# Ten of sixteen rows of summed mixing weights made in DRAM by copies and adding transfers, and one attention product tied to the end of z2

## The chip, the cores and the metric

The kernel runs on one core of a Trainium2 chip. A core has five engines that run their own instruction queues: TensorE (PE in the profile; its weight loads are PEld), VectorE (DVE), ScalarE (ACT), GpSimd (POOL) and SyncE (SP, which here only issues transfers). Transfers (DMA) are issued by SP, ACT or POOL and carried by 16 DMA engines. SBUF is the on-chip memory of 128 partitions, PSUM the accumulators that PE writes, DRAM the memory outside. The metric is the device time of one execution in microseconds, the median of several runs.

## The reference

The input x has 2048 rows of 512. It is normalised by rows to xn, and the result is x + s * silu(b), with

- s, attention: xn @ wqkv gives 32 heads of 16; each position looks at 8 earlier positions, 2 apart, with a softmax over these 8; the result goes through wo.
- b, a gated unit: z = gelu(xn @ w_in); z1 is its first 896 columns, z2 the other 896, normalised by rows; g = w_sp @ z2 + b_sp, where w_sp is 2048 x 2048 and mixes the rows (the "mixing"); b = (z1 * g) @ w_out.

```
z1 = z[..., :Fh]
z2 = _layernorm(z[..., Fh:], axis=-1)
g = jnp.einsum("ts,bsf->btf", w_sp, z2) + b_sp[None, :, None]
return jnp.einsum("bsf,fd->bsd", z1 * g, w_out)
```

All is float32. The kernel splits each operand of a product into a high and a low part (fp32r) and does three matmuls for one.

## The kernel before, in words

**Stages on PE.** In this order: the products of wqkv (until about 157 us), z1 (until about 226 us), z2 (until about 295 us), the mixing (twelve block products, until about 571 us), the product with w_out, and the product of attention's result with wo. Attention itself is DVE's work (16 units of two steps: scores L573, sums over a head L580, softmax, weighted product L620, folds, a transpose), with one fold on POOL (L633). It is issued at the lowest priority, its DVE instructions in one fixed order (`line`), and fills what the other work leaves free on DVE, from about 100 to 655 us. The scheduler of the framework orders each engine's instructions by priority and by a simulated timeline; `add_manual_dep` adds an edge, either only of order (NOSYNC) or one waited for at run time (SYNC).

**The mixing.** w_sp is cut into blocks of 128 x 512: four column groups c of outputs (512 each) by sixteen row blocks js. Two column groups belong to one half a (c = 2a, 2a + 1). For each half a and each pair of row blocks (i, 8 + i), the four blocks t0, t1 (row block i) and l0, l1 (row block 8 + i) take part in a scheme with seven products in place of eight (Strassen's, in Winograd's form), for which four sums of blocks are needed:

```
s3 = l1 + t1;  s1 = t1 + t0;  s0 = t0 + s3;  s2 = l0 + s0
```

So 2 halves x 8 = 16 rows of four sums. The plain blocks are used by the products m1, m2, m4 (`plain`), the sums by m6 (s0), m7 (s1), m5 (s3) and m3 (s2) (`summed`). They are made ahead and kept in DRAM (`sums_d`), each row by loading its four blocks, four additions (L393) and storing:

- half 1, rows 0 to 5: `pool_sums` on POOL, during the products of wqkv (L486 to L488); loads, additions and stores all on POOL.
- half 0, rows 0 to 7: `first_sums` during z1 (L690 to L715): loads on SP, additions on DVE, stores on POOL, in the t4 tiles.
- half 1, rows 6 and 7: `raw_sums` during z2 (L781): loads and stores on SP, additions on DVE, in the four raw buffers that also take the weights' loads.

**Weights.** `prep` (L175) fetches a block on SP into one of four raw buffers (`RAW = 4`), ACT makes the high part (L195) and DVE the low part (L197), in one of eight pairs of tiles. A raw buffer is free for the fetch four blocks on once the low part is made.

**z2.** For each i of eight, PE makes row blocks i and 8 + i in two halves of columns (`z2_half`, evicted by ACT at L733). One round later `z2_stats` counts mean and variance (DVE L742 to L745), POOL raises to the power -1/2 (L746) and makes the shift (L748); another round later ACT normalises (L754), ACT and DVE split, and `combine` (L767) makes the sums of z2 that the scheme needs.

**The start of the mixing.** m1a uses wsp_0 to wsp_7 of half 0 and z2's row blocks 0 to 7; m1b the same of half 1. Before m1b four PSUM banks get the bias by ACT (`seed`, L843). In `plain` a tie (L864 to L867) puts the tenth weighted product of attention (`sums_of[9]`, L620) on DVE behind the low part of wsp_6 of m1a.

Of the kernel before, what the change touches and what calls it, by code (L numbers as in the profile page):

```python
# [17 lines left out]
P = 128  # L18
# [6 lines left out]
FB = FH // P  # L25
# [3 lines left out]
JC = NT // NC  # L29
HT = NT // 2  # L30
F3 = 3 * P
ODD = 3
# [25 lines left out]
def kernel(  # L58
# [330 lines left out]

    def added(ts, eng):  # L390
        t0, t1, l0, l1 = ts
        for out_, p_, q_ in ((l1, t1, l1), (t1, t0, t1), (t0, t0, l1), (l0, t0, l0)):
            eng.tensor_tensor(out_, p_, q_, op=ALU.add)  # L393

    def block_sums(a, i, tile_=None, eng=nc.vector, loads=nc.sync, stores=nc.scalar, behind=None):
        top, low = [(tile_ or t4)(f"s{n}_{a}_{i}") for n in "ab"]
        for t, r in ((top, 0), (low, HT)):
            ins = loads.dma_start(t, w_sp[2 * a : 2 * a + 2, r + i].rearrange("c p t -> p c t"))
            if behind:
                tc.add_manual_dep(ins.ins, behind[0].ins.name, behind[1], reason="sums later")  # L400
        added([top[:, 0], top[:, 1], low[:, 0], low[:, 1]], eng)
        for r, t in enumerate((top, low)):
            stores.dma_start(sums_d[a, r, i], t)

    def raw_sums(a, i):
        ts = [
            fetch(w_sp[2 * a + c, r + i], CT, f"sr_{a}_{i}_{c}_{r}") for r in (0, HT) for c in range(2)
        ]
        added(ts, nc.vector)
        for n, t in enumerate(ts):  # L410
            nc.sync.dma_start(sums_d[a, n // 2, i, :, n % 2], t)

    def early_tile(name):
        return t2(name).rearrange("p (i t) -> p i t", i=2)

    def pool_sums(a, i, tile_, *behind):
        block_sums(a, i, tile_, nc.gpsimd, nc.gpsimd, nc.gpsimd, behind)

    z1_sums = [(0, i) for i in range(HT)]

# [57 lines left out]
    for j in range(11, NT):  # L478
        if j + 2 < NT:
            fetch_cols(j + 2)  # L480
        if j == NT - 3:
            rb = raws.tile([P, 512], F32, tag="raw", name="rb", bufs=RAW)
            rbv = rb.rearrange("p (j q) -> p j q", j=JC)
            pin(nc.sync.dma_start(rbv, mv_d[:JC, 1].unsqueeze(0).to_broadcast([P, JC, P])))
        turned = column_tile(j)
        if j == 12:  # L486
            for i in range(HT - 2):
                pool_sums(1, i, early_tile, turned, SYNC)  # L488
        low_x(j - 1, cols[j - 1])
        if j % 2:  # L490
            pair(0, j - 5)
# [197 lines left out]

    def first_sums(a, i):  # L690
        block_sums(a, i, stores=nc.gpsimd)

    first_sums(*z1_sums[0])

    for f in range(FB):
        pair_ = side_pair("w1_last") if f == FB - 1 else None
        wh, wl = prep(w_in1[:, f, :], KB * P, f"w1_{f}", pair_=pair_)
        for c in range(NC):
# [9 lines left out]
            zt = zp[:, c % 2]  # L708
            nc.scalar.activation(zt, pz, AF.Gelu_apprx_tanh)  # L709
            if c % 2:  # L710
                nc.scalar.dma_start(z1_d[f, c - 1 : c + 1].rearrange("c p t -> p c t"), zp)
# [13 lines left out]
    def z2_half(j, h, zt):  # L725
        xh, xl = xn_at(j)
        pz = mm(f"z2_{j}_{h}")[:, : WID[h]]
        for k in range(KB):
            wh, wl = [w[:, : WID[h]] for w in w2[k, h]]
            nc.tensor.matmul(pz, xh[:, k], wh, start=k == 0, stop=False)  # L730
            nc.tensor.matmul(pz, xh[:, k], wl, start=False, stop=False)  # L731
            nc.tensor.matmul(pz, xl[:, k], wh, start=False, stop=k == KB - 1)  # L732
        nc.scalar.activation(zt[:, HALF[h]], pz, AF.Gelu_apprx_tanh)  # L733

# [3 lines left out]
    def z2_stats(i, zts):  # L738
# [5 lines left out]
        mean, rstd = [mvz[:, i : i + HT + 1 : HT, n] for n in range(2)]  # L744
        nc.vector.tensor_scalar(rstd, rstd, EPS, None, op0=ALU.add)  # L745
        nc.gpsimd.tensor_tensor(rstd, rstd, nhalf.to_broadcast([P, 2]), op=ALU.pow)  # L746
# [101 lines left out]
    def block_product(a, name, z, w, odd=None, start=False, stop=False, steps=()):  # L848
        for n, s0 in enumerate(range(0, HT, 2)):
# [7 lines left out]
            for do in steps[n] if steps else ():  # L857
                do()

    def plain(a, c, r):  # L860
        def w(s):
            js = r * HT + s
            pair_ = spatial.get((2 * a + c, js)) or spatial_block(2 * a + c, js)
# [4 lines left out]
            return pair_  # L868
# [310 lines left out]
```

## Time and profile before

| | us |
|---|---|
| median of 3 runs | 695.89 (694.54 to 697.04) |
| the profiled execution, its own time | 696.54 |
| its span, first to last instruction | 694.8 |
| PE / DVE / ACT / POOL busy | 686.6 / 619.4 / 277.7 / 215.2 |
| DMA | 182.36 MB, mean 262 GB/s |

In rows of instructions the line, the engine, the operation and the tiles (out<-in) are given, with the start and the duration in us in a timeline, or with count, busy time and mean in a group; what stands in brackets is the idle time of the engine ahead of the instruction and what ended it. "SPq" is the issue of a transfer by SP. A row of waits gives the total, the number of times and the longest. A row of stretches gives the length, then each engine's busy time and number of instructions (PE, PEld, DVE, ACT, POOL), the granted clock, the share of the 16 DMA engines and GB/s. A row of one line's instructions gives the count, the shortest, median and longest duration in ns, and the first and last start. Matmuls overlap in the profile: one of 512 columns is drawn 0.39 us long, though the next starts earlier.

### The profile page before, as it was taken

How to read it: one execution, taken by the hardware profiler on the slowest of the kernel's cores; microseconds unless marked ns; L12 is line 12 of the kernel's file. 1: busy time of each engine (PE TensorE's matmuls, PEld its weight loads, DVE VectorE, ACT ScalarE, POOL GpSimd, SP SyncE). 2: the span in 40 equal slices, each digit the busy share in tenths (PEclk: the TensorE clock that was granted, in tenths of full speed). 3: DMA queues.
4: the chain of work that ended last, by engine and by line, in shares of the span. 5: the costliest groups of instructions: out<-in, count | busy, mean ns of one | idle time of the engine just before them, and what ended most of it. 6: DMA issues, size and time to landing. Idle time of an engine off the chain costs nothing.

```text
span 694.8 us, 9233 instructions
## 1 busy us (share of the span) xinstructions
PE 686.6 (99%) x3084; PEld 573.0 (82%) x3084; DVE 619.4 (89%) x866; ACT 277.7 (40%) x458; POOL 215.2 (31%) x242
## 2 busy tenths in 40 slices
PE   8999999999999999998999999999999999999998
PEld 7888888888888899986888888888888888888886
DVE  6776868999989989889999998999989999989775
ACT  4342234224424256865534544442334444211531
POOL 3104837372343322124123222223111201642320
PEclk9999999999999999999999999999999999999999
DMA  8769899969999865267899768667576692655796
GB/s 270 252 193 289 288 348 384 346 204 358 407 412 340 329 231 190 80 201 231 258 403 314 284 211 298 208 232 248 183 261 206 215 342 89 221 173 190 246 330 235
DMA packets 102223, 182.36 MB, mean 262 GB/s; under 512 B 9184, under 2 KB 45280, under 8 KB 102176
## 3 DMA queue, kind: packets, MB, share of 16 engines
q1 hardware_dynamic: 56624, 102.21, 43.6%
q0 software_dynamic: 13824, 52.24, 20.9%
q10 hardware_dynamic: 31728, 27.33, 11.7%
q8 instruction: 24, 0.39, 0.2%
q14 instruction: 23, 0.19, 0.1%
HBM read 122.42 MB, written 59.32 MB: 262 GB/s over the span
## 4 chain that ended last, share of the span: by engine, by line
PE 67%; DVE 13%; DMA 12%; ACT 3%; issue 3%; POOL 1%; SPq 1%; DVEq 0%; POOLq 0%; ACTq 0%
PE g L825 35%; PE b L1067 4%; PE b L1069 4%; PE b L1068 4%; PE qkv L387 4%; PE qkv L386 4%; PE qkv L385 4%; DMA sb<-in_w_sp 3%; PE s L1069 2%; PE s L1068 2%; PE s L1067 2%; DMA sums_d<-sb 2%; DVE zst L742 2%; DMA z_d<-z1t 1%; DVE xT L280 1%
## 5 line engine op out<-in xcount | busy, mean ns | idle before, releaser
L633 POOL TENSOR_TENSOR pv<-pv 128x1024 f32<-128x1024 f32 x29 | 69.6, 2399 | 96.2 <-DVE pv L620 85.9
L573 DVE TENSOR_TENSOR pr<-k,q 128x2048 f32<-128x2048 f32 x32 | 73.6, 2299 | 2.0 <-DMA k<-qkv_d 1.9
L620 DVE TENSOR_TENSOR pv<-v,lg 128x2048 f32<-128x2048 f32 x32 | 74.6, 2331 | 0.7
L580 DVE TENSOR_REDUCE lg<-pr 128x128 f32<-128x2048 f32 x32 | 73.0, 2281 | 0.1
L647 POOL DMA_DIRECT2D o_d<-tt x32 | 18.0, 562 | 138.9 <-DVE tt L646 103.8
L433 ACT ACTIVATE stage<-qkv 128x512 f32<-128x512 f32 x40 | 23.0, 590 | 30.8 <-DMA qkv_d<-stage 17.0
L807 POOL DMA_DIRECT2D ol<-o_d x32 | 17.7, 555 | 37.7 <-DVE BIG L197 11.1
L1078 ACT ACTIVATE bt<-b 128x512 f32<-128x512 f32 x16 | 9.4, 599 | 43.5 <-PE b L1069 39.4
L709 ACT ACTIVATE z1t<-z 128x512 f32<-128x512 f32 x28 | 15.5, 597 | 26.1 <-DMA z_d<-z1t 15.3
L280 DVE TENSOR_TENSOR xT<-xT,mr 128x512 f32<-128x512 f32 x20 | 14.9, 743 | 11.9 <-DMA mr<-mv_d 6.4
L732 PE MATMUL z<-w_0h,BIG 128*128 128x512 f32 x64 | 25.0, 391 | 0.0
L731 PE MATMUL z<-w_0l,BIG 128*128 128x512 f32 x64 | 25.0, 391 | 0.0
L730 PE MATMUL z<-w_0h,BIG 128*128 128x512 f32 x64 | 24.9, 390 | 0.0
L742 DVE BATCH_NORM_STATS2 zst<-zt 128x6 f32<-128x448 f32 x32 | 19.3, 613 | 6.1 <-ACT zt L733 6.0
L754 ACT ACTIVATE zt<-zt,nmz,mvz 128x896 f32<-128x896 f32 x16 | 17.5, 1129 | 18.0 <-POOL nmz L748 18.0
L638 DVE TENSOR_TENSOR pv<-pv 128x512 f32<-128x512 f32 x32 | 22.9, 716 | 0.0
L733 ACT ACTIVATE zt<-z 128x512 f32<-128x512 f32 (+1 forms) x32 | 15.9, 536 | 15.2 <-DMA sums_d<-sa 14.0
L732 PE MATMUL z<-w_1h,BIG 128*128 128x384 f32 x64 | 21.5, 336 | 0.0
L730 PE MATMUL z<-w_1h,BIG 128*128 128x384 f32 x64 | 21.5, 335 | 0.0
L731 PE MATMUL z<-w_1l,BIG 128*128 128x384 f32 x64 | 21.4, 335 | 0.0
L393 POOL TENSOR_TENSOR sb<-sa,sb 128x512 f32<-128x512 f32 x12 | 19.7, 1644 | 5.4 <-DMA sb<-in_w_sp 5.1
L195 ACT ACTIVATE BIG<-zl 128x512 fp32r<-128x512 f32 x20 | 12.5, 630 | 21.6 <-DVE zl L895 19.8
(478 smaller groups left out, 2296.2 us busy)
## 6 DMA issues: line engine op xcount, KB each, us to landing
qkv_d<-stage ACTq DMA_DIRECT2D x24, 512.0 KB
v<-qkv_d POOLq DMA_DIRECT2D x14, 704.0 KB, 5.4
k<-qkv_d POOLq DMA_DIRECT2D x13, 704.0 KB, 6.8
sums_d<-sa POOLq DMA_DIRECT2D x14, 512.0 KB, 7.8
sums_d<-sb POOLq DMA_DIRECT2D x14, 512.0 KB, 8.0
z_d<-z1t ACTq DMA_DIRECT2D x14, 512.0 KB
zl<-z_d SPq DMA_DIRECT2D x12, 512.0 KB
tr<-t_d SPq DMA_DIRECT2D x12, 384.0 KB
```

The source lines that it names most:

```text
L573: line(nc.vector.tensor_tensor(pr, taps(ks[u], j0), qb.unsqueeze(1).to_broadcast([P, W, NJ * CS]), op=ALU.mult))
L580: line(nc.vector.tensor_reduce(lgs[u][:, j0 * HS : (j0 + NJ) * HS].rearrange("p i w -> p w i"), pr.rearrange("p w (i d) -> p w i d", d=DH) ...
L620: line(nc.vector.tensor_tensor(pv.rearrange("p w (i d) -> p w i d", d=DH), taps(vs[u], j0).rearrange("p w (i d) -> p w i d", d=DH), lgs[u] ...
L633: eng.tensor_tensor(pv[:, 0:4], pv[:, 0:4], pv[:, 4:8], op=ALU.add)
L730: nc.tensor.matmul(pz, xh[:, k], wh, start=k == 0, stop=False)
L731: nc.tensor.matmul(pz, xh[:, k], wl, start=False, stop=False)
L732: nc.tensor.matmul(pz, xl[:, k], wh, start=False, stop=k == KB - 1)
L742: nc.vector.bn_stats(st[:, h], zt[:, h * FQ : (h + 1) * FQ])
L825: nc.tensor.matmul(pg, z[a], w[b], start=start and i == 0, stop=stop and i == 2, skip_group_check=seeded)
L1067: nc.tensor.matmul(pp[:, cols], hi, wh, start=k == 0, stop=False)
L1068: nc.tensor.matmul(pp[:, cols], hi, wl, start=False, stop=False)
L1069: nc.tensor.matmul(pp[:, cols], lo, wh, start=False, stop=k == n - 1)
```

## The change

The six rows on POOL stay (`MINE = 6`). The ten others (half 0, rows 0 to 7; half 1, rows 6 and 7) are made two rows at a time, as five pairs, without SBUF: for each pair four tensors in DRAM of 0.5 MB (`sums_q`), one for each sum. A sum is made by copying one block pair there (`copied`, issued by ACT) and adding another onto it with an adding transfer (`plus`, issued by POOL). `weight_sums` gives the 40 transfers in five rounds over the five pairs; `go_on(1, behind)` issues the next one, tied to the instruction `behind`: a copy by order on ACT alone, an adding transfer by a wait. It is called after each second eviction in z1 (14 times), after each row block of z2 (16 times) and after each pair of blocks in the mixing from m1b on (the last 10, so into m2b). All DVE additions and the SP loads and POOL or SP stores of these rows are gone. The tie of the tenth weighted product to wsp_6 is gone; instead the thirteenth (`sums_of[12]`) stands on DVE behind the last `z2_stats` (L745 of i = 7).

```diff
+MINE = HT - 2
+THEIRS = [(0, q) for q in range(HT // 2)] + [(1, q) for q in range(MINE // 2, HT // 2)]
...
-    sums_d = dram.tile([2, 2, HT, P, 2, CT], F32, name="sums_d")
+    sums_d = dram.tile([2, MINE, P, 2, CT], F32, name="sums_d")
+    sums_q = {
+        (a, n, q): dram.tile([2, P, CT], F32, name=f"sums_{a}_{n}_{q}")
+        for a, q in THEIRS
+        for n in range(4)
+    }
...
+    def rows_of_2k(blocks_):
+        return blocks_.rearrange("s p t -> (s p t)").rearrange("(r x) -> r x", x=4 * CT)
+
+    def raw_blocks(a, n, q):
+        r, c = divmod(n, 2)
+        j = r * HT + 2 * q
+        return w_sp[2 * a + c, j : j + 2]
+
+    def copied(to, a, q, src):
+        return nc.scalar.dma_start(rows_of_2k(sums_q[a, to, q]), rows_of_2k(src(a, q))), NOSYNC
+
+    def plus(to, a, q, src):
+        ins = nc.gpsimd.dma_start(
+            rows_of_2k(sums_q[a, to, q]), rows_of_2k(src(a, q)), accum_op=ALU.add, max_dma_last_dim=2048
+        )
+        return ins, SYNC
+
+    def weight_sums():
+        t0, t1, l0, l1 = [lambda a, q, n=n: raw_blocks(a, n, q) for n in range(4)]
+        s0, s3 = [lambda a, q, n=n: sums_q[a, n, q] for n in (0, 3)]
+        rounds = (
+            ((copied, 3, l1),),
+            ((copied, 0, t0), (plus, 3, t1)),
+            ((plus, 0, s3), (copied, 1, t0)),
+            ((plus, 1, t1), (copied, 2, l0)),
+            ((plus, 2, s0),),
+        )
+        for ops in rounds:
+            for a, q in THEIRS:
+                for fn, to, src in ops:
+                    yield fn, to, a, q, src
+
+    coming_sums = weight_sums()
+
+    def go_on(n, behind):
+        for fn, *args in itertools.islice(coming_sums, n):
+            ins, how = fn(*args)
+            tc.add_manual_dep(ins.ins, behind.ins.name, how, reason="sums paced")
...
-    first_sums(*z1_sums[0])
...
-            nc.scalar.activation(zt, pz, AF.Gelu_apprx_tanh)
+            out_of = nc.scalar.activation(zt, pz, AF.Gelu_apprx_tanh)
             if c % 2:
+                go_on(1, out_of)
                 nc.scalar.dma_start(z1_d[f, c - 1 : c + 1].rearrange("c p t -> p c t"), zp)
-        if f == 2:
-            first_sums(*z1_sums[FB])
-        if f < FB - 1:
-            first_sums(*z1_sums[f + 1])
...
-        nc.vector.tensor_scalar(rstd, rstd, EPS, None, op0=ALU.add)
+        known = nc.vector.tensor_scalar(rstd, rstd, EPS, None, op0=ALU.add)
+        if i == HT - 1:
+            tc.add_manual_dep(sums_of[12].ins, known.ins.name, NOSYNC, reason="gate rows ahead")
...
-        if i in (1, 3):
-            raw_sums(1, HT - 2 + i // 2)
...
-                    z2_half(j, h, zt)
+                    out_of = z2_half(j, h, zt)
+                    if h:
+                        go_on(1, out_of)
...
+            if name != "m1a":
+                go_on(1, highs[-1])
...
-            if (a, c, js) == (0, 0, 6):
-                tc.add_manual_dep(
-                    sums_of[9].ins, lows[-1].ins.name, NOSYNC, reason="first weights ahead"
-                )
...
     def summed(a, half_, i):
-        return lambda s: prep(sums_d[a, half_, s, :, i], CT, f"ws_{a}{half_}{i}_{s}")
+        def w(s):
+            if a and s < MINE:
+                src = sums_d[half_, s, :, i]
+            else:
+                src = sums_q[a, 2 * half_ + i, s // 2][s % 2]
+            return prep(src, CT, f"ws_{a}{half_}{i}_{s}")
+
+        return w
```

More of the change, by code (lines that the diff above doesn't have):

```diff
@@ L388, in product @@
         return pq
[L390 to L411, printed above, removed]
     def early_tile(name):
         return t2(name).rearrange("p (i t) -> p i t", i=2)
-    def pool_sums(a, i, tile_, *behind):
-        block_sums(a, i, tile_, nc.gpsimd, nc.gpsimd, nc.gpsimd, behind)
-    z1_sums = [(0, i) for i in range(HT)]
+    def pool_sums(i, *behind):
+        top, low = [early_tile(f"s{n}_{i}") for n in "ab"]
+        for t, r in ((top, 0), (low, HT)):
+            ins = nc.gpsimd.dma_start(t, w_sp[2:4, r + i].rearrange("c p t -> p c t"))
+            tc.add_manual_dep(ins.ins, behind[0].ins.name, behind[1], reason="sums later")
+        t0, t1, l0, l1 = [top[:, 0], top[:, 1], low[:, 0], low[:, 1]]
+        for out_, p_, q_ in ((l1, t1, l1), (t1, t0, t1), (t0, t0, l1), (l0, t0, l0)):
+            nc.gpsimd.tensor_tensor(out_, p_, q_, op=ALU.add)
+        for r, t in enumerate((top, low)):
+            nc.gpsimd.dma_start(sums_d[r, i], t)
@@ L486 @@
         if j == 12:
-            for i in range(HT - 2):
-                pool_sums(1, i, early_tile, turned, SYNC)
+            for i in range(MINE):
+                pool_sums(i, turned, SYNC)
         low_x(j - 1, cols[j - 1])
@@ L688 @@
     attention()
-    def first_sums(a, i):
-        block_sums(a, i, stores=nc.gpsimd)
-    first_sums(*z1_sums[0])
     for f in range(FB):
@@ L732, in z2_half @@
             nc.tensor.matmul(pz, xl[:, k], wh, start=False, stop=k == KB - 1)
-        nc.scalar.activation(zt[:, HALF[h]], pz, AF.Gelu_apprx_tanh)
+        return nc.scalar.activation(zt[:, HALF[h]], pz, AF.Gelu_apprx_tanh)
     def spatial_block(c, js):
@@ L862, in w @@
             js = r * HT + s
-            pair_ = spatial.get((2 * a + c, js)) or spatial_block(2 * a + c, js)
-            if (a, c, js) == (0, 0, 6):
-                tc.add_manual_dep(
-                    sums_of[9].ins, lows[-1].ins.name, NOSYNC, reason="first weights ahead"
-                )
-            return pair_
+            return spatial.get((2 * a + c, js)) or spatial_block(2 * a + c, js)
         return w
     def summed(a, half_, i):
-        return lambda s: prep(sums_d[a, half_, s, :, i], CT, f"ws_{a}{half_}{i}_{s}")
+        def w(s):
[5 more added lines that the diff above has]
+        return w
     def operand(i, s0):
```

## The prediction

> **What bounds the kernel now.** I read the page's busy times and chain first.
>
> ```profile
> span 694.8 us, 9233 instructions
> PE 686.6 (99%) x3084; PEld 573.0 (82%) x3084; DVE 619.4 (89%) x866; ACT 277.7 (40%) x458; POOL 215.2 (31%) x242
> ...
> PE 67%; DVE 13%; DMA 12%; ACT 3%; issue 3%; POOL 1%; SPq 1%; DVEq 0%; POOLq 0%; ACTq 0%
> ```
>
> TensorE (PE) is busy for 99% of the span and VectorE (DVE) for 89%; but a busy PE can hide gaps, so the next view is the list of PE's waits, and then the stretches of 25 us.
>
> ```profile
> PE g L825 <- ACT g L843: 1.9, 1, 1.9
> ...
> PE g L825 <- ACT BIG L195: 0.2, 1, 0.2
> ```
>
> ```profile
> 300.00:325.00 25.00, 22.89 (x100) 18.36 (x99) 22.84 (x32) 15.18 (x25) 8.34 (x9) 1.00 0.71 226
> 325.00:350.00 25.00, 25.00 (x111) 20.65 (x111) 25.00 (x35) 12.90 (x23) 6.44 (x6) 1.00 0.78 256
> ```
>
> After its opening PE waits in one place: the stretch from 300 to 325 us holds 100 matmuls of 512 columns where the next holds 111. That is where the mixing product begins. The matmuls around the hole:
>
> ```profile
> 314.66 0.39 PE L825 MATMUL g<-wsp_6l,BIG 128*128 128x512 f32 x1
> 314.89 0.39 PE L825 MATMUL g<-wsp_6h,BIG 128*128 128x512 f32 x1
> 317.17 0.50 PE L825 MATMUL g<-wsp_0h,BIG 128*128 128x512 f32 x1 [1.90 <-ACT g L843]
> ...
> 323.88 0.39 PE L825 MATMUL g<-wsp_3h,BIG 128*128 128x512 f32 x1
> 324.48 0.50 PE L825 MATMUL g<-wsp_7h,BIG 128*128 128x512 f32 x1 [0.21 <-ACT BIG L195]
> ```
>
> Starts are 0.23 us apart when PE flows (314.66 to 314.89). The first hole costs 317.17 - 314.89 - 0.23 = 2.05 us, the second 324.48 - 323.88 - 0.23 = 0.37 us, and the first matmul after each runs 0.50 instead of 0.39 us: 2.05 + 0.37 + 2 x 0.11 = **2.64 us**. This is all that any edit behind the opening can win before the last matmul; everything else it touches can at best stay hidden. Note the order: PE did the four products of row block 6, skipped block 7, went on to the second half (wsp_0 to wsp_3), and took wsp_7 at 324.48. The first hole waits for the seeds (L843), the second for z2's row block 7 (L195). What made both late stands on DVE, ScalarE (ACT), the load queue (SP) and GpSimd (POOL):
>
> ```profile
> 303.43 0.69 DVE L197 TENSOR_TENSOR wsp_6l<-wsp_6r,wsp_6h 128x512 fp32r<-128x512 f32 x1 [1.42 <-ACT wsp_6h L195]
> 304.04 2.29 DVE L620 TENSOR_TENSOR pv<-v,lg 128x2048 f32<-128x2048 f32 x1
> 306.24 2.28 DVE L580 TENSOR_REDUCE lg<-pr 128x128 f32<-128x2048 f32 x1
> ...
> 309.29 0.62 DVE L742 BATCH_NORM_STATS2 zst<-zt 128x6 f32<-128x448 f32 x1
> 309.82 0.67 DVE L197 TENSOR_TENSOR wsp_7l<-wsp_7r,wsp_7h 128x512 fp32r<-128x512 f32 x1
> ...
> 318.58 0.16 DVE L745 TENSOR_SCALAR mvz<-mvz 128x2 f32<-128x2 f32 x1
> ```
>
> ```profile
> 303.82 0.47 ACT L733 ACTIVATE zt<-z 128x384 f32<-128x384 f32 x1
> 304.20 0.62 ACT L195 ACTIVATE wsp_7h<-wsp_7r 128x512 fp32r<-128x512 f32 x1
> ...
> 313.99 0.64 ACT L195 ACTIVATE wsp_3h<-wsp_3r 128x512 fp32r<-128x512 f32 x1 [5.03 <-DMA wsp_3r<-in_w_sp]
> ...
> 316.00 0.63 ACT L195 ACTIVATE wsp_5h<-wsp_5r 128x512 fp32r<-128x512 f32 x1
> 316.53 2.14 ACT L843 ACTIVATE g<-b_bh 128x512 f32<-128x512 f32 x4
> 321.22 2.16 ACT L754 ACTIVATE zt<-zt,nmz,mvz 128x896 f32<-128x896 f32 x2 [2.54 <-POOL nmz L748]
> ```
>
> ```profile
> 310.52 0.33 SPq L169 DMA_DIRECT2D wsp_3r<-in_w_sp  x1
> ...
> 312.73 0.33 SPq L169 DMA_DIRECT2D wsp_5r<-in_w_sp  x1
> ```
>
> ```profile
> 318.82 1.68 POOL L746 TENSOR_TENSOR mvz<-mvz,nhalf 128x2 f32<-128x2 f32 x1 [1.83 <-DVE mvz L745]
> ```
>
> The tenth weighted product (L620) is tied behind wsp_6l, and runs at once at 304.04 with L580 behind it: 4.5 us. Meanwhile wsp_7h was done at 304.82, but wsp_7l came only at 309.82, and its raw buffer (there are four) lets wsp_3r start at 310.52, 0.03 us after. So wsp_3h is at 313.99; wsp_5r starts at 312.73, wsp_5h is at 316.00, and the seeds stand behind it on ACT. The same 4.5 us hold z2's last statistics (evicted at 304.29, counted at 309.29), and more attention holds L745 to 318.58.
>
> **The change part by part.** *DVE's sums.* Ten rows of four additions:
>
> ```profile
> L393 DVE TENSOR_TENSOR sb<-sa,sb x16: 627/684/1003, 169.3 to 244.1; 128x512 f32<-128x512 f32 x16
> ```
>
> 40 x 0.684 (the median of the commonest form) = 27.4 us leave DVE. On the path this is 0: PE has no wait there. The time goes to attention, which is next to be late on DVE.
>
> *The loads, stores and buffers of these rows.* SP loses 8 x 2 + 8 + 8 = 32 issues of about 0.33 us (the wsp_3r row), 10.6 us; POOL loses 16 store issues. 0 on the path, for the same reason.
>
> *Copies and adding transfers.* 40 of 0.524 MB: 20 copies issued by ACT, 20 adding ones by POOL, each pair of rows 4 + 4. Nearest rows for an issue:
>
> ```profile
> L711 ACTq DMA_DIRECT2D z_d<-z1t x14: 366/366/367, 160.6 to 223.3; - x14
> ...
> L403 POOL DMA_DIRECT2D sums_d<-sa x14: 532/545/589, 70.1 to 241.6; - x14
> ```
>
> ACT gains 20 x 0.366 = 7.3 us; by the order of the generator 10 copies fall in the z1 stage, 7 in z2, 3 later. POOL gains 20 x 0.545 and loses 16 x 0.545: +2.2 us. ACT is 40% and POOL 31% busy; if that cover were gone the cost is those 9.5 us at most. The trace has no transfer from DRAM to DRAM and none that adds. I bound one by what 0.524 MB takes at the full rate of the stretch 340 to 362 us below, 372 GB/s, so 1.41 us of all engines for a copy, and for an adding one 1.41 to 2.82 us (it carries at least the copy's bytes, at most twice them). I take the middle, 2.1, for lack of a nearer row. In the z1 stage 14 of them (7.3 MB) replace about 8 rows x 2.1 MB; the engines get relief. The 10 that come last (3 copies, 7 adds), in the first four products of the mixing, meet none of the removed work:
>
> ```profile
> 318.00:340.00 22.00, 21.79 (x96) 17.73 (x95) 21.96 (x39) 11.90 (x21) 6.56 (x6) 1.00 0.74 240
> 340.00:362.00 22.00, 22.00 (x98) 18.20 (x97) 21.90 (x27) 9.07 (x15) 7.11 (x7) 1.00 1.02 372
> 362.00:384.00 22.00, 22.00 (x98) 18.21 (x97) 20.60 (x26) 8.99 (x15) 6.60 (x8) 1.00 0.95 332
> 384.00:400.00 16.00, 16.00 (x72) 13.27 (x71) 15.86 (x24) 8.21 (x14) 3.87 (x3) 1.00 0.76 264
> ```
>
> Last but one number is the engines' share: free are 0.26 x 22 + 0 + 0.05 x 22 + 0.24 x 16 = 10.7 us. Needed are 3 x 1.41 + 7 x (1.41 to 2.82) = 14.1 to 24.0 us: more than is free by 3.4 to 13.3 us. What hides it: many transfers there (stores, attention's loads) are not urgent, and weights are split some us ahead of their use, the tightest being
>
> ```profile
> 392.05 0.68 DVE L197 TENSOR_TENSOR ws_5l<-ws_5r,ws_5h 128x512 fp32r<-128x512 f32 x1
> ```
>
> ```profile
> 394.65 0.39 PE L825 MATMUL g<-ws_5h,BIG 128*128 128x512 f32 x1
> ```
>
> 1.92 us. I cost it at 0 in the forecast, because they are paced 24 matmuls, 5.4 us, apart and weights need only 0.262 MB per 12 matmuls (2.7 us); 1.5 to 11.4 us if the weights take the whole excess less that lead.
>
> The Trainium skill, DMA: Bandwidth & Descriptors, "Rules for kernel authors", says that an accumulating DMA reads its destination before it writes it; counting that as half a copy more, an estimate, an add would take 2.1 us and the ten 19 us. The same page, "Issuing engines are not separate DMA queues", says that all issuing engines share the same 16 DMA engines; by that rule spreading the work over ACT and POOL wins nothing at a share of 1.02, which speaks for the second rival below.
>
> *The wait.* The tenth product loses its tie to wsp_6l; the thirteenth is tied behind L745 of the last z2 pair. Are twelve products done by then? DVE's products so far:
>
> ```profile
> 126.06 2.29 DVE L620 TENSOR_TENSOR pv<-v,lg 128x2048 f32<-128x2048 f32 x1
> ...
> 230.10 2.29 DVE L620 TENSOR_TENSOR pv<-v,lg 128x2048 f32<-128x2048 f32 x1
> ```
>
> ```profile
> 155.00:225.00 70.00, 70.00 (x312) 58.23 (x311) 67.33 (x88) 26.23 (x43) 24.92 (x29) 1.00 1.01 378
> 225.00:300.00 75.00, 75.00 (x374) 67.19 (x373) 67.00 (x133) 43.36 (x71) 18.14 (x30) 1.00 0.58 209
> ```
>
> These are the first and ninth: a step took at most 104.04 / 8 = 13.0 us, sums included; three more need under 39 us. There are 27.4 us plus the idle 2.7 + 8.0 us: 38. So they fit about, and nothing of attention is then left to stand on DVE before L745. Then, from the rows: eviction done 304.29; statistics 0.62 and L745 0.16 with a short aggregate between put L745's end near 305.6; from L746's start to L754's were 321.22 - 318.82 = 2.40 us, one L754 is 2.16 / 2 = 1.08, and the two splits some 0.62 + 0.68: row block 7 at about 310.4 instead of 324. PE had begun wsp_6 twelve matmuls before 315.1, at 312.4; in plain order it wants block 7 three matmuls later, at 313.1. If it is there, PE has 12 more matmuls, 2.7 us, ahead of the second half, so the seeds (the first done some 0.6 us after 316.53) are due at 317.8, not at 315.1. Bounds of this part: all 2.64 us won; or the attention freed at 305.5 holds wsp_7l as before and 0 is won. I take 2.3, leaving 0.3 for a first matmul after a short wait or a late split. Behind the thirteenth product stand L580, POOL's fold and the stores of attention; they start three steps further on than now, so the end of attention is earlier, not later.
>
> Sum: 0 + 0 + 0 - 2.3. The profiled execution took 696.54 us (span 694.8 and 1.7 around it), so 694.2 by its own time; the median of the runs shown is 695.89, so **693.6**.
>
> **The rivals.** *One: the hole comes back, no change, 695.9.* For it: the tie is freed at about 305.5, only 1.5 us after the 304.04 of now, and the chain raw buffer, load, ACT, seeds is untouched. Or twelve products aren't done, and the tie binds nothing. Against: row block 7 no longer waits for attention. *Two: slower, transfers crowd the weights out.* Place: the blocks from 340 to 400 us. It decides once the ten last transfers take over 10.7 + 1.9 = 12.6 us from the weights alone. At the middle price, 19.0 - 12.6 = 6.4 us lost: 693.6 + 6.4 = 700.0. Against: 101% of the engines' time in the z1 stage (the 155 to 225 row) made PE wait for nothing. *Three: slower, POOL's order.* An adding transfer paced by the second pair of weights (wsp_3h, now 313.99) stands ahead of the last L746 on POOL; then block 7 is ready near 314.6 + 0.5 + 2.4 + 1.1 + 1.3 = 319.9, and PE, in plain order, waits 6.8 us: 700.4. Against: L746 is ready about 9 us before that.
>
> **How the numbers follow.** Forecast 0.50 (own range 692.9 to 694.5); rival one 0.24; two 0.18; three 0.08. 0.3% of 695.89 is 2.1 us, about what a measurement here can tell from no change: faster means under 693.8. Of the forecast 0.38 lies there and 0.12 within; rival one is within; two and 0.06 of three are slower, 0.02 within. Faster 0.38, same 0.38, slower 0.24. The range goes from the whole 2.64 us and half a us of scatter, 692.7, to the middle of rival two, 700.1.
>
> **What would show it.** Right: no wait of PE on L843 or L195 near 315, L745 before 308 us, PE in the order wsp_6, wsp_7, wsp_0, twelve L620 before L745. Wrong: new PE waits on L195 between 340 and 400 with ACT waiting for weight loads (rival two); L746 behind an adding transfer (three); or a hole of 2 us at the same seeds (one). A hole anywhere before 295 us would break the claim that the removed work was all hidden.

## The result and the profile after

| | before | after |
|---|---|---|
| median | 695.38 us (4 runs beside it) | 733.79 us (4 runs, 731.02 to 734.76) |
| ratio | | 1.0543 (95% interval 1.0507 to 1.0579) |
| profiled execution, its span | 696.54, 694.8 | 731.02, 729.2 |

The changed kernel is slower by 38 us; 693.6 and a range up to 700.1 were forecast. Line numbers have moved: L423 is the adding transfer (`plus`), L420 the copy, L649 the weighted product of attention (L620 before), L662 POOL's fold behind it (L633), L667 VectorE's fold behind that (L646), L754 z2's eviction (L733), L766 the last of z2's statistics (L745), L777 its normalisation (L754), L790 its sums (L767), L848 the mixing (L825), L202 and L204 the high and low parts of a split (L195, L197). In the kernel before, z1 starts at 141.66 us (L703) and z2 at 217.8, some 15 and 8 us earlier than the text on its stages says: the forecast's row from 155 to 225 us leaves out the first 13 us of z1 and takes in the first 7 of z2.

The page's head and queues, and the list of PE's waits, both of after:

```profile
span 729.2 us, 9134 instructions
PE 695.4 (95%) x3084; PEld 577.8 (79%) x3084; DVE 598.5 (82%) x826; ACT 283.8 (39%) x462; POOL 227.1 (31%) x246
...
q0 software_dynamic: 16960, 54.34, 26.5%
q10 hardware_dynamic: 32368, 37.82, 15.4%
...
PE 61%; DVE 14%; DMA 10%; issue 10%; POOL 2%; ACT 2%; ACTq 0%; POOLq 0%; DVEq 0%; SPq 0%
```

```profile
PE g L848 <- DVE wsp_12l L204: 13.3, 1, 13.3
PE g L848 <- ACT wsp_1h L202: 6.3, 1, 6.3
PE z L752 <- DVE lg L627: 3.1, 1, 3.1
PE z L751 <- ACT zt L754: 2.3, 2, 1.3
PE g L848 <- DVE wsp_1l L204: 1.5, 1, 1.5
```

PE falls from 99% to 95% of a longer span, and "issue" rises from 3% to 10% of the chain. The hole that the forecast wanted to win, PE's wait for the seeds, is gone; new waits stand in its place, the five longest of which are shown. The first product with w_out starts at 605.52 in place of 570.77: of these 34.8 us, 7.0 are lost by the start of the mixing (302.12 in place of 295.13) and 27.8 in it. Behind that nothing more is lost (the spans differ by 34.4).

**The longest hole, 390 to 404 us.** The timeline of PE, of DVE and of POOL around it:

```profile
390.37 0.39 PE L848 MATMUL g<-wsp_12h,BIG 128*128 128x512 f32 x1
404.08 0.79 PE L848 MATMUL g<-wsp_12l,BIG 128*128 128x512 f32 x1 [13.32 <-DVE wsp_12l L204]
...
409.18 0.39 PE L848 MATMUL g<-wsp_12h,BIG 128*128 128x512 f32 x1
```

```profile
401.54 0.69 DVE L667 TENSOR_TENSOR pv<-pv 128x512 f32<-128x512 f32 x1 [21.03 <-POOL pv L662]
...
403.35 0.68 DVE L204 TENSOR_TENSOR wsp_12l<-wsp_12r,wsp_12h 128x512 fp32r<-128x512 f32 x1
```

```profile
367.00 0.97 POOL L423 DMA_DIRECT2D sums<-sums  x1 [5.15 <-ACT BIG L202]
376.88 0.91 POOL L423 DMA_DIRECT2D sums<-sums  x1 [8.92 <-issue]
386.01 0.88 POOL L423 DMA_DIRECT2D sums<-sums  x1 [8.23 <-issue]
391.79 0.89 POOL L423 DMA_DIRECT2D sums<-sums  x1 [4.89 <-issue]
397.66 0.88 POOL L423 DMA_DIRECT2D sums<-sums  x1 [4.97 <-issue]
...
398.84 2.67 POOL L662 TENSOR_TENSOR pv<-pv 128x1024 f32<-128x1024 f32 x1
```

Read it from the bottom. The last five adding transfers stand in a row on POOL. Each next one waits 5 to 9 us for its issue; POOL takes its instructions in order, so what stands behind waits too. POOL's fold starts at 398.84, though its product was done at 375.5; VectorE, in order, has waited 21.03 us for it at L667; behind L667 stands the low part of the next weight; PE waits 13.32 us for that. What each issue waits for can be read off the row of the line, taken over all twenty adding transfers:

```profile
DMA to landing us min/median/max: 5.4/6.2/10.7
```

They land between 5.4 and 10.7 us after their issue, and the distances of the last five issues are 9.88, 9.13, 5.78 and 5.87 us: the queue goes on about when the transfer before has landed.

**The hole at the start of the mixing, 302.58 to 309.25 us**, on SP, DVE and ACT:

```profile
290.27 0.33 SPq L815 DMA_DIRECT2D b_a<-in_b_sp  x1
```

```profile
296.85 0.69 DVE L1033 TENSOR_TENSOR b_a<-b_a 128x512 f32<-128x512 f32 x1 [3.11 <-DMA b_a<-in_b_sp]
```

```profile
302.99 0.52 ACT L202 ACTIVATE BIG<-zt 128x384 fp32r<-128x384 f32 x1 [3.30 <-DVE zt L790]
...
308.58 0.63 ACT L202 ACTIVATE wsp_1h<-wsp_1r 128x512 fp32r<-128x512 f32 x1
```

The second weight block of the mixing stands on ACT behind z2's normalisations; these wait for VectorE, which waited 3.11 us for a load of the bias. In the kernel before, that load is issued at 275.8 and VectorE does not wait for it.

**The stretches** show what else is lost (columns as before; x is the number of matmuls, then the granted clock, the share of the DMA engines):

```profile
155.00:225.00 70.00, 69.53 (x309) 57.55 (x308) 58.20 (x69) 26.01 (x41) 23.29 (x24) 1.00 0.91 300
225.00:300.00 75.00, 70.14 (x338) 62.67 (x339) 68.58 (x113) 37.89 (x59) 32.57 (x37) 0.98 0.81 204
300.00:325.00 25.00, 17.21 (x66) 13.69 (x65) 21.52 (x42) 17.25 (x28) 6.60 (x9) 0.80 0.81 219
...
400.00:425.00 25.00, 20.16 (x77) 15.77 (x78) 21.71 (x32) 10.81 (x18) 8.83 (x10) 0.82 0.89 289
```

From 225 to 300 us the share of the engines is 0.81 where it was 0.58. The granted clock falls behind each long hole: from 404.08 to 409.18 us PE starts eleven matmuls, 0.43 us apart for the most part, where eleven take 2.5 us at 0.23. That is some 2.6 us on top of the 13.3. By the Trainium skill, TensorE: Matmul & The Clock Gate, Part 1: The HAM clock gate, the array falls to half of its clock when it has idled for about 3.4 us and needs about as long of sustained activity to get it back; the halving agrees with 0.43 against 0.23, the time here was 5.1 us.

### The profile page after: what moved, and what is told of

The parts are those of the page before. It is cut to its first block, busy times and chain, and to the rows that moved or that the text cites. A ratio compares the mean times of both kernels' runs of the same rounds, so it can differ in the third digit from the quotient of the medians.

```text
span 729.2 us, 9134 instructions
## 1 busy us (share of the span) xinstructions
PE 695.4 (95%) x3084; PEld 577.8 (79%) x3084; DVE 598.5 (82%) x826; ACT 283.8 (39%) x462; POOL 227.1 (31%) x246
## 4 chain that ended last, share of the span: by engine, by line
PE 61%; DVE 14%; DMA 10%; issue 10%; POOL 2%; ACT 2%; ACTq 0%; POOLq 0%; DVEq 0%; SPq 0%
PE g L848 24%; PE qkv L392 5%; PE qkv L394 5%; PE qkv L393 5%; DMA v<-qkv_d 4%; PE b L1096 3%; PE b L1094 3%; PE b L1095 3%; DVE lg L609 3%; PE s L1096 2%; PE s L1094 2%; PE s L1095 2%; DVE pr L602 2%; PE qkv L315 2%; DVE pv L649 2%
## 5 line engine op out<-in xcount | busy, mean ns | idle before, releaser
L662 POOL TENSOR_TENSOR pv<-pv 128x1024 f32<-128x1024 f32 x29 | 70.1, 2418 | 86.7 <-DVE pv L649 74.8
L649 DVE TENSOR_TENSOR pv<-v,lg 128x2048 f32<-128x2048 f32 x32 | 74.5, 2329 | 11.5 <-DMA v<-qkv_d 10.9
L676 POOL DMA_DIRECT2D o_d<-tt x32 | 18.7, 583 | 135.4 <-DVE tt L675 104.2
L667 DVE TENSOR_TENSOR pv<-pv 128x512 f32<-128x512 f32 x32 | 22.9, 717 | 21.1 <-POOL pv L662 21.0
L777 ACT ACTIVATE zt<-zt,nmz,mvz 128x896 f32<-128x896 f32 x16 | 17.6, 1128 | 27.1 <-POOL nmz L771 27.1
L635 ACT ACTIVATE lg<-lg 128x256 f32<-128x256 f32 x16 | 6.6, 410 | 53.7 <-DVE lg L630 53.7
L1155 DVE TENSOR_TENSOR sg<-s,sg 128x512 f32<-128x512 f32 (+2 forms) x17 | 11.2, 659 | 15.5 <-PE s L1096 15.3
L423 POOL DMA_DIRECT2D sums<-sums x10 | 9.2, 924 | 45.9 <-issue 27.0
```

What stands on the lines that cost most here:

```text
L649: line(nc.vector.tensor_tensor(pv.rearrange("p w (i d) -> p w i d", d=DH), taps(vs[u], j0).rearrange("p w (i d) -> p w i d", d=DH), lgs[u] ...
L662: eng.tensor_tensor(pv[:, 0:4], pv[:, 0:4], pv[:, 4:8], op=ALU.add)
```

## The experiments

Times are medians; a ratio stands against the kernel before of the same batch, whose medians were 694.6 to 695.8; kernels with one run have no interval.

**One: how the parts add up.** Four kernels put the change together piece by piece: the sums of VectorE gone; then the new tie; then the issues; then the whole transfers, and last the adding. First, VectorE's sums gone and the old tie.

```diff
-        for fn, *args in itertools.islice(coming_sums, n):
+        for fn, *args in ():
...
-                src = sums_q[a, 2 * half_ + i, s // 2][s % 2]
+                src = raw_blocks(a, 2 * half_ + i, s // 2)[s % 2]
```

and the tie of the kernel before:

```diff
-            tc.add_manual_dep(sums_of[12].ins, known.ins.name, NOSYNC, reason="gate rows ahead")
...
+                tc.add_manual_dep(
+                    sums_of[9].ins, lows[-1].ins.name, NOSYNC, reason="first weights ahead"
+                )
```

> As the last one, but with the tie of the kernel before (tenth weighted product behind the low part of the eighth spatial block): VectorE's sums taken away and nothing put in their place, which is the gain that the prediction counted on. The prediction's reading: 2.3 us under the kernel before, 692 to 694 us. Rival, VectorE's free time only lets attention run ahead into loads and into POOL's fold, in order, so that splits are late all the same: 696 to 705 us.

693.40 us, ratio 0.9973 (0.9962 to 0.9985). (The tie is the one to wsp_6, the seventh block.)

```profile
PE 686.1 (99%) x3084; PEld 574.1 (83%) x3084; DVE 599.7 (87%) x826; ACT 280.0 (40%) x458; POOL 206.2 (30%) x226
```

PE has no wait behind its opening. The gain that the forecast counted on exists, 1.6 us of the 2.3 that it took; it comes when VectorE's sums go, with their loads and stores, and does not need the new tie. Whether VectorE's time or the relieved DMA engines bring it is not told apart. Next, the same with the new tie.

> The changed kernel with none of the forty transfers: the products that read summed weights load the raw blocks of the same size instead (the sums, and so the output, are not computed). The tie of the thirteenth weighted product behind z2's last statistics stays, VectorE's sums are gone. Theory one, all of the 38 us come from the transfers (POOL's queue and the engines): the time falls to the kernel before, 693 to 698 us. Rival, the 18 us that were left with plain copies come from the tie and from where attention's work now falls: 707 to 714 us, with the hole of 5 us near 300 still there. Between them, 699 to 706, the part left is shared.

699.81 us, 1.0058 (1.0030 to 1.0085), between the two theories, as the case of shared parts: the tie costs 6.4 us here, and the transfers are most of the 38 us but not all.

```profile
PE g L848 <- DVE wsp_1l L204: 1.8, 1, 1.8
...
PE g L848 <- ACT wsp_1h L202: 1.3, 1, 1.3
```

Then the forty transfers at their places, each of one row, while the products still load the raw blocks:

```diff
-        return nc.scalar.dma_start(rows_of_2k(sums_q[a, to, q]), rows_of_2k(src(a, q))), NOSYNC
+        return nc.scalar.dma_start(rows_of_2k(sums_q[a, to, q])[:1], rows_of_2k(src(a, q))[:1]), NOSYNC
...
-            rows_of_2k(sums_q[a, to, q]), rows_of_2k(src(a, q)), accum_op=ALU.add, max_dma_last_dim=2048
+            rows_of_2k(sums_q[a, to, q])[:1], rows_of_2k(src(a, q))[:1], accum_op=ALU.add, max_dma_last_dim=2048
```

> The changed kernel with all forty transfers issued at their places, the adding ones still adding, but each of one 2 KB row in place of 256 (64 for the copies of 8 KB rows); the products load the raw blocks, so the sums and the output are not computed. It has the issues on POOL and ScalarE and their waits for evictions, and neither the engine time nor the descriptors. Theory, engine time and descriptor places make the 34 us between the changed kernel and the one without transfers (699.8): 700 to 703 us, with no wait of POOL for an issue over 1 us. Rival, the places of the issues in POOL's queue, behind evictions, make a part: 706 to 714 us.

702.21 us, 1.0116 (1.0093 to 1.0140); no adding transfer waits for its issue. Issues and their waits for evictions cost 2.4 us, and PE's first wait of the mixing is longer than the 1.3 us without them:

```profile
PE g L848 <- ACT wsp_1h L202: 3.9, 1, 3.9
```

Then the whole transfers, those of POOL without adding:

```diff
-            rows_of_2k(sums_q[a, to, q]), rows_of_2k(src(a, q)), accum_op=ALU.add, max_dma_last_dim=2048
+            rows_of_2k(sums_q[a, to, q]), rows_of_2k(src(a, q)), max_dma_last_dim=2048
```

> The kernel after with GpSimd's 20 transfers made plain copies of the same rows, without the adding (the summed weights are then not the sums; nothing else is left out); same order. Theory Q, with places taken by the reads of both operands: a plain copy takes half of the places, two or three are in flight at once, and the time falls to 700 to 715 us. If 256 rows alone fill the space, or if the bytes written are what counts: 725 to 735 us.

712.99 us (one run; sums not computed). The longest of PE's waits and the queue of POOL's transfers:

```profile
PE g L848 <- ACT wsp_1h L202: 5.1, 1, 5.1
```

```profile
q0 software_dynamic: 14400, 54.34, 21.5%
```

The hole at 390 is gone, and the waits of these transfers for an issue fall from 33.5 us in all to 6.2; the hole at the start of the mixing stays. So, in this order: before 694.97; sums off VectorE -1.6; new tie +6.4; issues +2.4; full transfers +10.8; adding +20.8; after 733.79. Each is a difference of two medians, most of them from different batches, and the kernel without adding has one run: by the ratios the issues cost 4.0 and the full transfers 9.1 us. The prices hold for this order only, and the framework's scheduler orders VectorE's instructions somewhat differently where the loads do not read the sums (the second and third kernel against the fourth), so that a part of +2.4 and +10.8 may be its work.

What a transfer costs the engines is estimated from the pages, as if the other transfers of a queue took as long in each kernel; no run shows that, and a packet's time may hold waiting where the engines are crowded. The queue's share times the span is 193.2 us after, 0.215 x 711.2 = 152.9 without adding, and without the transfers

```profile
q0 software_dynamic: 11520, 43.85, 18.4%
q10 hardware_dynamic: 31728, 27.33, 12.0%
```

0.184 x 696.8 = 128.2. A plain transfer of POOL thus takes (152.9 - 128.2) / 20 = 1.2 us of all 16 engines, an adding one (193.2 - 128.2) / 20 = **3.25 us**, and a copy of ACT (0.154 x 729.2 - 0.120 x 696.8) / 20 = 1.4 us.

**Two: the tie, alone and left out.**

On the kernel before, only the tie changed:

```diff
+            tc.add_manual_dep(sums_of[12].ins, known.ins.name, NOSYNC, reason="gate rows ahead")
...
-                tc.add_manual_dep(
-                    sums_of[9].ins, lows[-1].ins.name, NOSYNC, reason="first weights ahead"
-                )
```

> The kernel before with the tie of the kernel after alone: the thirteenth weighted product behind the last z2 statistics, in place of the tenth behind wsp_6; VectorE still makes the sums. Theory Q: the tie is not what costs; 692 to 699 us, with or without the hole of 2 us at the start of the mixing. Rival P (the tie): attention's twelve steps ahead of the mixing hold VectorE up, holes at 224 and 302 us as in the kernel after; over 705 us.

712.88 us, 1.0248 (1.0226 to 1.0270).

```profile
PE g L827 <- ACT BIG L195: 6.9, 4, 2.8
```

```profile
250.00:300.00 50.00, 46.86 (x220) 41.52 (x220) 48.91 (x93) 25.38 (x40) 20.68 (x24) 0.93 0.53 173
```

The three products that the old tie held back now lie beside z2, with the sums; VectorE is busy for 48.91 of 50 us, where it was 42.24 before, and z2's splits are late.

The changed kernel with the same edit undone (its first line out, its last three in):

> The kernel after with the tie of the kernel before: the tenth weighted product behind the low part of wsp_6, nothing behind the last z2 statistics; the sums stay in DRAM. What is known: the tie alone, on the kernel before, cost 17 us, and the whole change 38. Theory Q+P (two causes that hardly touch each other): the tie goes, the holes near 302 us (some 11 us with the slow matmuls behind them) go, those of GpSimd's adding transfers stay: 708 to 722 us. If only the transfers cost (Q alone): 728 to 736 us. If the tie is what lets five adding transfers stand in a row (P alone): 695 to 702 us.

738.94 us, 1.0637 (1.0616 to 1.0659), above all three ranges.

```profile
PE g L846 <- DVE wsp_13l L204: 18.2, 1, 18.2
```

The DRAM sums alone cost 44 us, and on top of them the new tie wins 5, where alone it costs 17 (or 6.4 with VectorE free): the two edits do not add. The longest hole is the same chain through POOL, here 18.2 us.

**Three: how much of it is POOL's queue.** More room for the descriptors of POOL's transfers:

```diff
-    nc = _bacc.Bacc("TRN2", target_bir_lowering=False, num_devices=1, dynamic_dma_scratch_size=1024)
+    nc = _bacc.Bacc("TRN2", target_bir_lowering=False, num_devices=1, dynamic_dma_scratch_size=1152)
```

> The kernel after with 1152 in place of 1024 bytes per partition for GpSimd's descriptors, the most that fits in SBUF; every engine's order is the same. Theory Q: if one adding transfer takes 33 of 64 places on each ring, two fit in 72 and not in 64, so the wait ahead of a lone second one goes, and in the row of five each waits for the last but one: GpSimd is held some 15 to 20 us in place of 36, and the time falls to 705 to 722 us. Theory T: 730 to 735 us.

722.73 us, 1.0394 (1.0369 to 1.0419). An eighth more room takes more than half of the waits of the changed kernel, and of its hole; the time falls by 11 us, just above the 705 to 722 of theory Q. First that kernel's row, then the two of this one:

```profile
POOL sums L423 <- issue: 33.5, 8, 8.9
```

```profile
POOL sums L423 <- issue: 15.5, 4, 7.2
```

```profile
PE g L848 <- DVE wsp_12l L204: 5.2, 1, 5.2
```

Rows of 8 KB in place of 2 KB, so 64 rows in place of 256:

```diff
-            rows_of_2k(sums_q[a, to, q]), rows_of_2k(src(a, q)), accum_op=ALU.add, max_dma_last_dim=2048
+            rows_of_2k(sums_q[a, to, q]), rows_of_2k(src(a, q)), accum_op=ALU.add, max_dma_last_dim=8192
```

> The kernel after, with the adding transfers cut into 64 rows of 8 KB in place of 256 rows of 2 KB; same bytes, same sums, the same order of instructions on every engine. Theory Q (queue): in the kernel after, GpSimd issues an adding transfer only about 0.3 us after the transfer before it has landed (376.54 and 376.88, 385.68 and 386.01 us), because the rows of one such transfer take up most of the space for descriptors; five in a row held GpSimd's queue from 362 to 398 us, and with it the fold, VectorE and TensorE. With a quarter of the rows the wait of 5 to 9 us ahead of each adding transfer falls under 1 us and the time to 695 to 702 us. Theory T (traffic): the bytes crowd the engines; unchanged, 730 to 735 us.

724.25 us, 1.0418 (1.0395 to 1.0442). No adding transfer waits for an issue any more, but the time falls by 10 us only, far from the 695 to 702 of theory Q:

```profile
373.44 9.59 SPq L176 DMA_DIRECT2D wsp_14r<-in_w_sp  x1
```

```profile
392.96 0.63 ACT L202 ACTIVATE wsp_12h<-wsp_12r 128x512 fp32r<-128x512 f32 x1 [9.84 <-DMA wsp_12r<-in_w_sp]
```

All five now run at once, and loads of weights take their place in the crowd: ACT waits 9.84 us for one, and SP's issue itself takes 9.59 us in place of 0.33; from 350 to 400 us the share of the engines is 1.03 to 1.04. Cut the one cause, and the other, hidden by it, is met.

Half as many adding transfers in a stretch, the last five one per two pairs of blocks:

```diff
-            if name != "m1a":
+            if name != "m1a" and (name in ("m1b", "m2a") and paced[0] < 5 or n % 2):
+                paced[0] += 1
```

> The kernel after with the last five adding transfers paced half as densely, so that three and not five stand in a row on GpSimd between two folds of attention. Theory Q: GpSimd is held some 16 to 20 us less there and the hole of 13.5 us at 390 us, with the slow matmuls behind it 16.8 us, falls under 3 us: 716 to 722 us. Theory T (traffic): 728 to 735 us.

725.12 us (one run), between the two theories. The waits of these transfers for an issue are 32.5 us in all, against 33.5, but the fold now stands behind three of the last five and starts at 386.14. The hole at 390 is small, and others have come, of which this is the longest:

```profile
PE g L849 <- DVE ws_1l L204: 4.6, 1, 4.6
```

At last, the link between POOL and VectorE, cut:

```diff
-            first_fold(part, nc.gpsimd if coming else nc.vector)
+            first_fold(part, nc.vector)
```

> The changed kernel with the first fold of every weighted product on VectorE instead of POOL, so that no work of VectorE stands behind POOL's adding transfers; the transfers are as they are. If the chain adding transfer, POOL's fold, VectorE's next fold, low part of a weight, TensorE is what makes the hole of 13.5 us at 390, that hole falls under 3 us and the time to 715 to 724 us, though VectorE gets some 28 folds of about 1.4 us (twice the 0.717 us of the second fold, which has half the elements). If the engines' traffic makes it, the hole stays over 8 us and the time is 728 to 740 us.

728.69 us, 1.0479 (1.0446 to 1.0513). Each theory was half right. The hole at 390 went, as the first said; the time stayed in the range of the second, since the waits of these transfers for an issue grew to 58.3 us and VectorE met the next thing that stands on POOL behind the adding transfers, the store of attention's result (L676), whose buffer the transpose (L675) needs:

```profile
408.68 0.45 DVE L675 STREAM_TRANSPOSE tt<-pv 128x256 f32<-128x256 f32 x1 [14.42 <-DMA o_d<-tt]
```

```profile
417.98 0.79 PE L848 MATMUL g<-ws_0l,BIG 128*128 128x512 f32 x1 [16.77 <-DVE ws_0l L204]
```

So it is the queue and not the fold.

**Four: the hole that was to be won.** Two edits of the kernel before, on the tenth product's tie. First, behind the low part of wsp_7:

```diff
-            if (a, c, js) == (0, 0, 6):
+            if (a, c, js) == (0, 0, 7):
```

> The kernel before with the tenth weighted product tied behind the low part of wsp_7 in place of wsp_6, nothing else. My reading of the hole of 2.05 us at 315 us was that this product and the reduction behind it (304.0 to 308.5 us) hold wsp_7's low part, its raw buffer and so the loads and the seeds. If that is so the hole goes and the time falls by 1.5 to 2.6 us, to 693 to 694.5. If the scheduler's order makes the hole elsewhere: within 1 us of before, or slower by up to 5.

698.84 us, 1.0058 (1.0043 to 1.0072), and the wait for the seeds grew from 1.9 us:

```profile
PE g L825 <- ACT g L843: 3.5, 1, 3.5
```

The time went the other way, yet the trace bears out the chain. wsp_7l comes at 303.74 in place of 309.82, and wsp_3r is fetched at 304.44 in place of 310.52. The product and its reduction now hold the next low part, wsp_0l, and with its raw buffer the load of wsp_4r (issued at 311.15), behind which the seeds stand:

```profile
304.80 2.29 DVE L620 TENSOR_TENSOR pv<-v,lg 128x2048 f32<-128x2048 f32 x1
...
310.45 0.68 DVE L197 TENSOR_TENSOR wsp_0l<-wsp_0r,wsp_0h 128x512 fp32r<-128x512 f32 x1
```

```profile
315.97 0.63 ACT L195 ACTIVATE wsp_4h<-wsp_4r 128x512 fp32r<-128x512 f32 x1 [6.05 <-DMA wsp_4r<-in_w_sp]
```

One weight later the product does the same harm one weight further on.

Then behind z2's last L745, in place of the weight:

```diff
+            tc.add_manual_dep(sums_of[9].ins, known.ins.name, NOSYNC, reason="gate rows ahead")
```

> The kernel before with the tenth weighted product (not the thirteenth) tied behind the last z2 statistics, in place of behind wsp_6; sums by VectorE. It has the new place of the tie without the three more steps. If the three more steps of attention inside z2's stage are what cost 17 us (rival P), the loss goes: 693 to 698 us. If the place behind the statistics costs: 705 to 714 us.

696.62 us, 1.0033 (1.0020 to 1.0046). The hole is gone, L745 stands at 306.02 us, near the 305.6 of the working, and the mixing takes 568.86 - 294.94 = 273.9 us in place of 275.6; but the last stage, in which PE waits 0.6 us for a split of attention's result (o_3h), loses as much:

```profile
568.86 0.39 PE L1065 MATMUL b<-wout_0h,BIG 128*128 128x512 f32 x1
...
690.87 0.28 PE L1067 MATMUL s<-BIG,o_3l 128*128 128x128 f32 x1
```

Before, these stand at 570.77 and 691.02. What makes the last stage longer was not isolated; attention's last transpose (L646) starts at 659.96, earlier than the 663.89 of before. Rival P is borne out: with the tie at the same place, the three more steps beside z2 make 712.88 us out of 696.62.

**Five: the sums on POOL's arithmetic**, with no transfer in DRAM. Six of the ten rows of the kernel before, then two:

```diff
-        added(ts, nc.vector)
+        added(ts, nc.gpsimd)
...
-        block_sums(a, i, stores=nc.gpsimd)
+        block_sums(a, i, eng=nc.gpsimd if i % 2 else nc.vector, stores=nc.gpsimd)
```

> The kernel before with six of VectorE's ten sums computed on POOL (every second one beside z1 and the two beside z2); all transfers and their queues as before. It asks whether the 1.6 us that VectorE's free time is worth can be had by a queue that does not wait on transfers. If POOL's four additions of 1.3 to 1.6 us only delay the folds by as much: 693 to 695 us. If VectorE's next fold waits for POOL as in the changed kernel, at a smaller size: 696 to 700 us.

706.85 us, 1.0180 (1.0156 to 1.0203).

```profile
PE g L825 <- ACT wsp_1h L195: 6.8, 1, 6.8
```

> As the last one with only the two sums beside z2 on POOL, where POOL is busy for 3 to 4 of 25 us but also forms z2's rstd and shift. If VectorE's time beside z2 is what the hole at the start of the mixing needs: 693.5 to 695 us. If the rstd on POOL comes late by the additions' 1.3 to 1.6 us each: 696 to 699 us.

With the first edit only: 701.11 us, 1.0093 (1.0071 to 1.0115), and 2.7 us of wait at the same place. Both are slower, by more than was expected, and by the hole at the start of the mixing that the changed kernel has too, with and without its transfers. ACT's order there is the same in these kernels and in the one before: the second weight stands behind z2's sixth normalisation, whose row blocks wait for VectorE and POOL. What comes to stand in that chain is different in each; I read it from the trace and did not isolate it. The wait for the bias, for one, is 2.5 us in the second kernel and absent in the first, whose hole is longer.

VectorE's time was not even freed. In the first kernel it is busy for 631.5 us, against 619.4 before, though 24 of its 40 additions are gone; some of its instructions take far longer from 200 to 245 us, where POOL adds, most of all

```profile
208.01 7.37 DVE L573 TENSOR_TENSOR pr<-k,q 128x2048 f32<-128x2048 f32 x1
...
238.48 4.74 DVE L601 TENSOR_TENSOR lg<-lg,mx 128x256 f32<-128x256 f32 x1
```

where the medians of these lines are 2.28 and 0.42 us. No run tells what makes them long.

## Why the prediction was wrong, by its own steps

- **What bounds the kernel**: right as far as it goes. PE waited in one place, and no kernel won more there than the 2.64 us. But the removed sums were costed at 0, and with them gone, the old tie kept and nothing added, the hole closes and 1.6 us are won: the gain was booked on the tie and comes here without it.
- **Loads and stores removed, issues moved, at 0**: the new issues with their waits cost 2.4 us (4.0 by the ratios). On POOL one took 0.92 us (the page's mean for L423), not the 0.545 of a store.
- **Price of an adding transfer**: about 3.25 us of all engines, outside the bounds of 1.41 to 2.82; the argument "at most twice the bytes" does not bound it, since descriptors of 2 KB are dearer here when they add: the same rows without adding took 1.2. With rows of 8 KB it is (0.251 x 721.6 - 128.2) / 20 = 2.65 us, from this row of that kernel:

```profile
q0 software_dynamic: 13120, 54.34, 25.1%
```

  The Trainium skill, DMA: Bandwidth & Descriptors, "Rules for kernel authors", has the destination read before it is written; the estimate of half a copy more that I took from it made 2.1, too low as well. The copy's 1.41 was right.
- **"I cost it at 0 ... because they are paced 24 matmuls, 5.4 us, apart"**: this is the step that failed, and most of the 38 us: full transfers and their adding cost 31.6 us (10.8 + 20.8) in place of 0. The pace of the evictions says when a transfer may start, not when the queue is free again. A second adding transfer stands on POOL until the first has landed (5.4 to 10.7 us), and everything behind it stands too: fold, stores, attention's loads. That held VectorE for 21.03 and PE for 13.32 us at 390. It was read as work on the engines alone, with a loss up to 11.4 us; its place in an order was left out.
- **Relief in the z1 stage**: right there (0.91 in place of 1.01 of the engines from 155 to 225 us), but over all the engines carry more. Removed are (0.209 x 694.8 - 128.2) = 17 us on POOL's queue and (0.436 x 694.8 - 0.378 x 696.8) = 40 on SP's (shares of q0 and q1 before and without transfers), 57 in all; added 20 x 3.25 + 20 x 1.4 = 93.
- **The tie, -2.3**: wrong in sign where nothing is added in DRAM, +6.4 with VectorE free and +17 alone; on top of the transfers it wins 5. Twelve products did fit (the twelfth runs at 259.54), but that was not the condition: they fit by running beside z2, and make its chain late. L766 of the last pair came at 323.35 us, not before 308. With nine products ahead in place of twelve, L745 does come where the working had it (306.02 for 305.6), and the hole goes.
- **Rivals**: two (crowding, 700.0) is there, in the kernel with rows of 8 KB, at 340 to 400 us as described. Its size was too low, and not by the price alone: with 2.65 its own sum is 3 x 1.4 + 7 x 2.65 - 12.6 = 10.2 us, and that kernel is 22 above the one with issues only. Three had the queue right and the follower wrong: not z2's rstd (L746) but the fold, and behind it VectorE. It was priced for one transfer; five in a row stand there. The statement "a hole anywhere before 295 us would break the claim" came true in the changed kernel, 3.1 us at 224, 1.3 and 0.9 us near 260; but with the sums removed and nothing else there is no such hole, so it was not the removed work that made them.

**What stays open**: how the 31.6 us divide between queue and engines. With the waits for an issue gone (rows of 8 KB) 724 us are left, without adding 713; the two hide one another. Open is, too, which wait of z2's chain sets the hole at the start of the mixing. No kernel that makes the sums beat the one before; the one with VectorE's sums left out, 693.40, shows how little was to be had.

## What to carry to other kernels

Before work is moved to an engine's transfers, ask what stands behind them on that engine's queue and who waits for it in order; how long a transfer keeps the queue counts as well as how long it keeps the engines. Price an unknown transfer by running one, since here an adding transfer took 2.6 times a plain one. An engine relieved of work gains little where nothing much waits for it, here 1.6 us, and the work that moves into its free time may stand in front of what is urgent.

## What the runs showed of the hardware

- An adding transfer of 256 rows of 2 KB holds back the next adding transfer of GpSimd until about its landing, 5.4 to 10.7 us (33.5 us of waits for an issue in all); with an eighth more room for descriptors 15.5 us are left, without adding 6.2, in 64 rows none. A store right behind the last of the row was issued at once (398.21).
- It takes some 3.25 us of all 16 engines for 0.5 MB, in 8 KB rows 2.65, a plain one 1.2 to 1.4, by the estimate from the queues' shares.
- SP's issue of a load took 9.59 us, not 0.33, with five adding transfers in flight.
- After a hole of 13 us TensorE ran at about half its pace for 5.1 us.
- With 24 of VectorE's additions moved to GpSimd, VectorE was busy for 12 us longer, and not 16 us shorter (24 x 0.684).
